# A diffusion transformer block on one core: LayerNorm tile 2's statistics and transposes moved ahead of K, one K pair split, and the last store's waits reordered

## The chip, the core and the metric

One core of one Trainium2 chip. The metric is the time of one execution on the device in microseconds (us); each kernel is run several times, and the median is told. A profile is one execution; its span is some 1.4 us shorter than the time of the same run. Times within a profile count from the start of its span.

Two kinds of number come from a trace here. Starts and durations of instructions are as the profile's views give them. Completions ("done") and landings are the semaphore updates in the trace, counted against the program's own order: every instruction of this kernel adds one to its engine's semaphore, and every transfer adds sixteen to its own. The n-th update therefore names its instruction. That is finer than the merged views and was needed for differences of a tenth of a microsecond.

## The reference

```python
B, N, D = (2, 256, 1152)          # 512 tokens in 4 tiles of 128; F = 4608, 2 heads of 576
mod = (_silu(c) @ w_mod).reshape(B, 6, 1, D)
shift_a, scale_a, gate_a, shift_m, scale_m, gate_m = [mod[:, i] for i in range(6)]
h = _layernorm(x, axis=-1) * (1 + scale_a) + shift_a
qkv = (h @ wqkv).reshape(B, N, 3, H, Dh)
# attention, wo, gate, second LayerNorm and modulation, two MLP matmuls with GELU, gate   [cut]
```

The change touches only the first line of h, the start of K, and the last store.

## The kernel before

The program is written in units with a small scheduler. TensorE and the store queue follow source order; VectorE and ScalarE follow a fixed list for the head. An instruction waits for exactly what it reads or overwrites; PSUM, the memory that TensorE writes to, is tracked by bank. Weights come in slices in a fixed order on one queue: x of both batches, three slices of the scale weights for feature blocks 0 to 3 (called slices 0, 1, 2 here), the first four rows of K's weights, three slices of the scale weights for blocks 4 to 8 (the second half), the other five K rows, and so on.

LayerNorm statistics: tiles 1 and 2 on VectorE, tiles 0 and 3 on ScalarE, the power -0.5 on GpSimd, the normalization (xn) on VectorE:

```python
def ln_stats_dve(src, chunks, bn_t, mv_t, rstd_t, tag):      # tiles 1, 2
    # three bn_stats, bn_aggr, + EPS on VectorE                              [cut]
    pool(650, ... tensor_tensor(out=rstd_t, in0=var, in1=NHALF, op=ALU.pow), "rstd_" + tag)
# ln_stats_act: tiles 0, 3: sum and square sum on ScalarE, variance, the same power  [cut]
```

TensorE ahead of K. `warm` is a matmul of 512 columns without use (in the profile of before the first ones start some 427 ns apart, from 6.74 on 216); `xn_T` transposes a normalized tile, `sca` sums one slice of the scale (three rows of weights, twelve matmuls of two columns), `hk` multiplies K's operand by the scale:

```python
XB = [(4, 5, 3), (6, 5, 7)]            # PSUM banks of the transposes, by batch
KB = [(0, 1, 2, 3), (4, 5, 6)]         # PSUM banks of the K pairs
        xn_T(1)
        warm(1, "c")
        sca(0, 3)
        xn_T(0)
        warm(1, "d")
        sca(3, 6)
        warm(1, "e")
        sca(6, 9)
        hk(0, 0)
        # ...                                                                [cut]
        xn_T(3, 0, 8)
        k_first(0)                     # a round of K: 8 matmuls of 256 columns
        k_first(1)
        xn_T(3, 8, 9)
        xn_T(2)
        # k_first(2), k_first(3), hk of batch 1, two K pairs of batch 1      [cut]
        sc_ones(KC, KT)
        k17(0, 0, KC)                  # four matmuls of K's last column block
        for kt in range(KT):
            mod_kt(WSC, kt, 0, "scb_%d" % kt, (KC, KT))     # second-half scale sums
        hk(KC, 0)
        # ...                                                                [cut]
        k_pair(range(KC), 2, 1)        # 8 matmuls; then the second half of K
```

The last store first waits for the oldest stores, then for VectorE:

```python
                    if ins is last_out:
                        for o in outs[:-4]:
                            eng_handle.wait_ge(dma_sems[o.dma_sem], o.dma_val)
                    for (k, v) in waits[ins.gidx]:
                        # wait for it                                        [cut]
```

Of the kernel before, what the change touches and what calls it, by code (L numbers as in the profile page):

```python
# [171 lines left out]
class Sched:  # L172
# [225 lines left out]
    def emit(self, nc, sems, dma_sems):  # L398
        order = self.order
        eidx = {e: 0 for e in ENGINES}  # L400
        dma_cnt = [0] * len(dma_sems)
        n_other = getattr(self, "n_other_dma_sems", 8)
        n_sp = len(dma_sems) - n_other
        di = 0
        dj = 0
        for e in ENGINES:
            for u in order[e]:
                for ins in u.instrs:
                    if u.dma_bytes > 0:
                        if e == "sp":  # L410
                            k = di % n_sp
                            di += 1
                        else:
                            k = n_sp + dj % n_other
                            dj += 1
                        dma_cnt[k] += 16
                        ins.dma_sem = k
                        ins.dma_val = dma_cnt[k]
                    else:
                        eidx[e] += 1  # L420
                        ins.eidx = eidx[e]
        self.final_counts = dict(eidx)
        self.final_dma = list(dma_cnt)
        snap = {}
        stats = {"waits": 0}

        def sem_of(d):
            if d.dma_sem is not None:
                return ("d", d.dma_sem), d.dma_val
            return ("e", d.unit.eng), d.eidx  # L430

        allu = sorted(self.units, key=lambda u: (u.start, u.uid))
        known = {e: {} for e in ENGINES}
        waits = {}
        for u in allu:
            e = u.eng
            kn = known[e]
            for ins in u.instrs:
                need = {}
                for d in ins.deps:  # L440
                    k, v = sem_of(d)
                    if need.get(k, 0) < v:
                        need[k] = v
                wl = []
                for k, v in sorted(need.items(), key=lambda kv: (-kv[1], str(kv[0]))):
                    if kn.get(k, 0) >= v:
                        continue
                    wl.append((k, v))
                    kn[k] = v
                    for d in ins.deps:  # L450
                        if sem_of(d) == (k, v):
                            sn = snap.get(d.gidx)
                            if sn:
                                for kk, vv in sn.items():
                                    if kn.get(kk, 0) < vv:
                                        kn[kk] = vv
                            break
                waits[ins.gidx] = wl
                stats["waits"] += len(wl)
                snap[ins.gidx] = dict(kn)  # L460
        self.wait_stats = stats

        outs = [ins for u in order["sp"] for ins in u.instrs if ins.is_out]
        last_out = outs[-1]

        def run_engine(e, eng_handle):
            for u in order[e]:
                for ins in u.instrs:
                    if ins is last_out:
                        for o in outs[:-4]:  # L470
                            eng_handle.wait_ge(dma_sems[o.dma_sem], o.dma_val)
                    for (k, v) in waits[ins.gidx]:
                        if k[0] == "d":
                            eng_handle.wait_ge(dma_sems[k[1]], v)
                        else:
                            eng_handle.wait_ge(sems[k[1]], v)
                    bi = ins.fn(eng_handle)
                    if ins.dma_sem is not None:
                        bi.then_inc(dma_sems[ins.dma_sem], 16)
                    else:  # L480
                        bi.then_inc(sems[e], 1)
            if e == "sp":
                for o in outs[-4:-1]:
                    eng_handle.wait_ge(dma_sems[o.dma_sem], o.dma_val)
                eng_handle.wait_ge(dma_sems[last_out.dma_sem], last_out.dma_val)

        for e, eng in (("sp", nc.sync), ("pe", nc.tensor), ("act", nc.scalar), ("dve", nc.vector), ("pool", nc.gpsimd)):
            run_engine(e, eng)
# [12 lines left out]
KT = 9  # L501
# [8 lines left out]
KC = 4  # L510
# [3 lines left out]
def c_mm(n):  # L514
    return max(n / 2.4 + 2.5, 27.0)
# [26 lines left out]
def build_kernel(nc, x, c, wqkv, wo, w_mod, w_fc1, w_fc2, out):  # L542
    S = Sched()
# [4 lines left out]
    with (  # L548
# [10 lines left out]
        def ps32(bank, c0=0, n=512):  # L559
            return psum[:, bank * 512 + c0: bank * 512 + c0 + n]  # L560
# [47 lines left out]
        Q4B = sb(O_Q4B, 1024)  # L608
# [18 lines left out]
        IDENT = sb(misc(256), 256)  # L627
# [59 lines left out]
        def mm(o, l, r, st, sp, **kw):  # L687
            S.instr(lambda e: e.matmul(o, lhsT=l, rhs=r, start=st, stop=sp, **kw), reads=[l, r], writes=[o])  # L688
# [73 lines left out]
                [xt, m, rs], [xn], "xn_%d" % t)  # L762


        XB = [(4, 5, 3), (6, 5, 7)]

        def xslot(b, kt, n=256):
            return ps16(XB[b][kt // 4], (kt % 4) * 256 + (512 if kt == 8 and b == 1 else 0), n)
# [2 lines left out]
        def xn_T(t, ka=0, kb=KT):  # L771
            b = t // 2
            S.unit("pe", (kb - ka) * c_mm(128), "xnT_%d_%d" % (t, ka))
            for kt in range(ka, kb):
                tr(xslot(b, kt)[:, (t % 2) * 128:(t % 2) * 128 + 128], XN[:, t, kt * 128:(kt + 1) * 128], IDENT)
# [5 lines left out]
        def warm(n, tag, behind=None):  # L781
            for i in range(n):
                S.unit("pe", 300.0, "warm_%s_%d" % (tag, i))
                mm(ps32(2), IDENT, Q4B, True, True)
                if behind:
                    S.instrs[-1].deps.update(j for j in S.instrs[:-1] if j.name == behind)

        def mod_kt(W, kt, col0, name, fs=(0, 9)):
            S.unit("pe", (fs[1] - fs[0]) * 27.0, name)
            for f in range(*fs):  # L790
                mm(ps32(7, col0 + f * 2, 2), W[:, kt, f * 128:(f + 1) * 128], ST[:, kt:18:9], False, kt == KT - 1, skip_group_check=True)
# [16 lines left out]
        def k_mm(kts, j, b, bank, half):  # L808

            for kt in kts:  # L810
                mm(ps32(bank, half * 256, 256), WK[:, kt, j * 128:(j + 1) * 128], HK[:, kt, b * 256:(b + 1) * 256], kt == 0 and half == 0,
                   kt == KT - 1, skip_group_check=True)

        KB = [(0, 1, 2, 3), (4, 5, 6)]
        ev_rr = [0]

        def k_pair(kts, i, b, bank=None):
# [25 lines left out]
        for n, behind in ((1, "bn_ln1_1_1"), (1, "aggr_ln1_1"), (2, "veps_ln1_1"), (2, "rstd_ln1_1")):  # L843
            warm(n, behind, behind)
        xn_T(1)
        warm(1, "c")
        sca(0, 3)
        xn_T(0)
        warm(1, "d")
        sca(3, 6)  # L850
        warm(1, "e")
        sca(6, 9)
        hk(0, 0)
        sc1a(0, KC)
# [7 lines left out]
        def k_first(kt):  # L862
            for i in range(4):
                k_pair((kt,), i, 0)

        k_first(0)
        k_first(1)
        xn_T(3, 8, 9)
        xn_T(2)
        xn_T_copy(1, 4, 8, "act")  # L870
        xn_T_copy(1, 8, 9, "act")
        for kt in range(2, KC):
# [6 lines left out]
        def k17(b, ka, kb):  # L879
            S.unit("pe", (kb - ka) * c_mm(256), "k17_%d_%d" % (b, ka))  # L880
            for kt in range(ka, kb):
                mm(ps32(7, 256 * (1 - b), 256), WK[:, kt, D - P:D], HK[:, kt, b * 256:(b + 1) * 256], b == 1 and kt == 0, kt == KT - 1,
                   skip_group_check=True)

        sc_ones(KC, KT)
        k17(0, 0, KC)
        for kt in range(KT):
            mod_kt(WSC, kt, 0, "scb_%d" % kt, (KC, KT))
        hk(KC, 0)
        sc1a(KC, KT)  # L890
        for kt in range(KC, KT):
            for b in range(2):
                if kt > KC or b:
                    hk(kt, b)
        k_pair(range(KC), 2, 1)
        for kt in range(KT):
            dma(WQ[:, kt, :], wqkv_v[:, kt, 0:D], P * D * 2, "ld_wq%d" % kt, run=2304)
            dma(WSM[:, kt, :], wmod_v[:, kt, 4 * D:5 * D], P * D * 2, "ld_sm%d" % kt, run=2304)
# [43 lines left out]
        for kt in range(KT):  # L942
            for b in range(2):
# [5 lines left out]
                else:  # L949
# [4 lines left out]

        S.first = {
            "dve": ["zq4b", "c_half", "c_silu", "bn_ln1_1_0", "bn_ln1_1_1", "bn_ln1_1_2", "aggr_ln1_1", "veps_ln1_1", "bn_ln1_2_0",
                    "xn_1", "bn_ln1_2_1", "xn_0", "bn_ln1_2_2", "aggr_ln1_2", "var_ln1_3", "veps_ln1_2", "xn_3", "hk_0_0", "sc1a_0", "hk_1_0",
                    "xn_2", "hk_0_1", "hk_1_1", "hk_2_1", "hk_3_1", "hk_%d_0" % KC, "sc1a_4", "hk_%d_1" % KC] + ["hk_%d_%d" % (kt, b) for kt in range(KC + 1, KT) for b in range(2)],
            "act": ["ld_c", "c_tanh", "sum_ln1_0", "sq_ln1_0", "sum_ln1_3", "sq_ln1_3", "xnT_cp0_4", "xnT_cp0_8", "hk_2_0", "hk_3_0",
                    "xnT_cp1_4", "xnT_cp1_8"],  # L960
        }
# [293 lines left out]
        for t in range(4):  # L1255
            b = t // 2
# [3 lines left out]
            for (c0, c1) in pieces:  # L1260
                w = c1 - c0
                S.unit("pe", JT * c_mm(w), "fc2_%d_%d" % (t, c0))
                o = ps32(acc_bank(), 0, w)
# [8 lines left out]
        by = {u.name: u for u in S.units}  # L1272
# [1 line left out]
            if u.eng == "dve" and u.name.startswith("h2T_3"):  # L1274
                S.order_after(by["gm_0_0"], u)
        S.order_after(by["gm_1_0"], by["gm_0_8"])
        S.order_after(by["rstd_ln1_2"], by["rstd_ln1_3"])
        for u in S.units:
            if u.eng == "dve" and u.name.startswith("hx_"):
                S.order_after(by["sm_0_0"], u)  # L1280
# [64 lines left out]
```

## Time and profile before

| | before |
|---|---|
| time, median of 3 runs | 244.39 us (244.12 to 244.48) |
| span of the profile | 243.0 us |
| TensorE busy | 238.2 us (98%) |
| slice 1, slice 2 landed | 9.54, 10.75 |
| first K matmul | 11.80 |
| third slice of the second half landed | 18.53 |
| first matmul of the second half of K | 20.16 |
| VectorE's last update, last store starts | 241.333, 241.431 |

TensorE is the bound almost throughout. In such a profile the only things worth looking for are TensorE's waits, and work on it that could be done while it waits. The lines are in the prediction.

### The profile page before, as it was taken

The numbers are of one execution on the slowest core, as the hardware profiler recorded it, in microseconds if no ns is written. First come the engines' busy times: TensorE is split into PE (matmuls) and PEld (weight loads), VectorE is DVE, ScalarE is ACT, GpSimd is POOL, SyncE is SP. The second block draws the span as 40 slices with busy tenths as digits, with TensorE's granted clock in tenths as the row PEclk, the third lists the DMA queues.
The fourth block names the chain that finished last, engine by engine and source line by source line (L and its number), as shares of the span: only waits on it lengthen the run. The fifth ranks groups of instructions, "written<-read, shape, count | busy, mean of one in ns | idle before, by whom it ended". The sixth has DMA issues, their size and how long they took to land.

```text
span 243.0 us, 4065 instructions
## 1 busy us (share of the span) xinstructions
PE 238.2 (98%) x1753; PEld 148.0 (61%) x1763; DVE 120.4 (50%) x217; ACT 67.2 (28%) x136; POOL 21.5 (9%) x39
## 2 busy tenths in 40 slices
PE   7999999999999999999999999999999999999996
PEld 2698854556667666898444444444656656666575
DVE  3724379596997899789999600000022222111112
ACT  4730350345424206983233322222000000000000
POOL 1500000000021186400000000020000000000000
DMA  6999999999995999979953498011000000000000
GB/s 237 334 381 392 392 391 391 398 414 405 389 350 170 350 386 393 392 266 392 323 162 82 166 308 323 0 32 68 0 16 19 16 16 19 16 16 19 18 28 21
DMA packets 30140, 51.59 MB, mean 212 GB/s; under 512 B 1703, under 2 KB 15787, under 8 KB 30123
## 3 DMA queue, kind: packets, MB, share of 16 engines
q1 hardware_dynamic: 29680, 50.14, 57.7%
q0 software_dynamic: 416, 1.19, 1.6%
q8 instruction: 14, 0.23, 0.4%
q14 instruction: 3, 0.02, 0.0%
q10 hardware_dynamic: 27, 0.00, 0.0%
HBM read 50.14 MB, written 1.19 MB: 211 GB/s over the span
## 4 chain that ended last, share of the span: by engine, by line
PE 94%; DMA 3%; SPq 1%; issue 0%; DVE 0%
PE psum L688 93%; DMA arena<-in_w_mod_dram 3%; PE psum L691 1%; SPq L669 1%; DVE arena L805 0%; DVE arena L1268 0%; DVE arena L1269 0%
## 5 line engine op out<-in xcount | busy, mean ns | idle before, releaser
L688 PE MATMUL psum<-arena 128*128 128x384 bf16 (+12 forms) x1664 | 234.8, 307 | 2.4 <-POOL arena L711 1.5
L688 PEld LDWEIGHTS psum<-arena 128*128 128x128 bf16 (+3 forms) x1674 | 142.7, 97 | 90.6 <-issue 4.5
L1063 DVE SCALAR_TENSOR_TENSOR arena<-arena 128x1152 f32<-128x1152 bf16 x32 | 44.7, 1414 | 0.6
L1268 DVE TENSOR_TENSOR arena<-psum,arena 128x384 f32<-128x384 f32 (+3 forms) x14 | 7.0, 501 | 68.0 <-PE psum L688 68.0
L1177 ACT ACTIVATE arena<-psum 128x512 bf16<-128x512 f32 (+1 forms) x44 | 22.4, 520 | 42.7 <-PE psum L688 42.7
L683 ACT ACTIVATE arena<-psum 128x512 bf16<-128x512 f32 (+6 forms) x37 | 19.6, 550 | 38.6 <-PE psum L688 37.0
L685 DVE CAST arena<-psum 128x512 bf16<-128x512 f32 (+3 forms) x13 | 8.2, 641 | 11.4 <-PE psum L688 11.3
L669 POOL DMA_DIRECT2D dit_scratch<-arena x3 | 1.8, 617 | 115.6 <-DVE arena L685 58.8
L1145 POOL TENSOR_TENSOR arena<-arena 128x384 f32<-128x384 f32 x12 | 10.9, 914 | 11.4 <-DVE arena L1144 9.8
L1090 DVE CAST arena<-psum 72x32 bf16<-72x32 f32 x1 | 0.2, 187 | 21.3 <-PE psum L688 21.3
L739 DVE BATCH_NORM_STATS2 arena<-arena 128x6 f32<-128x384 f32 (+1 forms) x18 | 9.5, 548 | 0.1
L1150 ACT ACTIVATE arena<-arena 128x1152 bf16<-128x1152 f32 x4 | 5.3, 1344 | 11.1 <-DVE arena L1149 11.1
L1144 DVE TENSOR_TENSOR arena<-psum,arena 128x384 f32<-128x384 f32 x12 | 6.5, 552 | 1.5 <-PE psum L688 0.9
L1269 DVE TENSOR_TENSOR arena<-arena 128x384 bf16<-128x384 f32 (+3 forms) x14 | 7.0, 501 | 0.5
L691 PE MATMUL psum<-arena 128*128 128x128 bf16 (+1 forms) x89 | 7.1, 219 | 0.0
L691 PEld LDWEIGHTS psum<-arena 128*128 128x128 bf16 (+1 forms) x89 | 5.8, 98 | 2.0 <-DMA arena<-in_c_dram 0.8
L1167 ACT ACTIVATE arena<-psum,arena 128x128 bf16<-128x128 bf16 x16 | 6.0, 456 | 1.7 <-PE psum L691 1.1
L1164 DVE TENSOR_SCALAR arena<-psum,arena 128x128 bf16<-128x128 bf16 x20 | 5.4, 336 | 1.9 <-PE psum L691 1.9
L1070 DVE TENSOR_REDUCE arena<-arena 128x36 f32<-128x1152 f32 x4 | 5.4, 1346 | 0.0
L1067 DVE STREAM_TRANSPOSE arena<-arena 128x1152 f32<-128x1152 f32 x4 | 5.4, 1363 | 0.0
L993 ACT ACTIVATE arena<-psum,arena 128x256 bf16<-128x256 f32 x8 | 3.7, 473 | 1.3 <-PE psum L688 0.9
L947 ACT ACTIVATE arena<-arena 128x256 bf16<-128x256 bf16 x6 | 2.6, 498 | 3.9 <-DVE arena L941 3.9
(48 smaller groups left out, 45.8 us busy)
## 6 DMA issues: line engine op xcount, KB each, us to landing
arena<-in_w_fc_dram SPq DMA_DIRECT2D x9, 1152.0 KB, 7.5
arena<-in_w_fc_dram SPq DMA_DIRECT2D x4, 2592.0 KB, 17.4
arena<-in_wqkv_dram SPq DMA_DIRECT2D x18, 288.0 KB, 10.3
arena<-in_w_mod_dram SPq DMA_DIRECT2D x3, 1728.0 KB, 20.4
arena<-in_w_mod_dram SPq DMA_DIRECT2D x3, 864.0 KB, 13.3
arena<-in_w_mod_dram SPq DMA_DIRECT2D x9, 288.0 KB, 10.8
arena<-in_wqkv_dram SPq DMA_DIRECT2D x1, 2592.0 KB, 16.7
arena<-in_wo_dram SPq DMA_DIRECT2D x1, 2592.0 KB, 24.4
```

The source lines that it names most:

```text
L683: act(c_act(n), lambda e: e.activation(out=dst, in_=src, func=ACTF.Copy), [src], [dst], name)
L685: dve(c_dve_psum16(n) if psum16 else c_dve_psum32(n), lambda e: e.tensor_copy(dst, src), [src], [dst], name)
L688: S.instr(lambda e: e.matmul(o, lhsT=l, rhs=r, start=st, stop=sp, **kw), reads=[l, r], writes=[o])
L691: S.instr(lambda e: e.transpose(o, i_, idn), reads=[i_, idn], writes=[o])
L739: dve(550, lambda e, s=s, o=o: e.bn_stats(out=o, in_=s), [s], [o], "bn_%s_%d" % (tag, ci))
L1063: dve(1270, lambda e, w=w, s=s, acc=acc: e.scalar_tensor_tensor(out=acc, in0=w, scalar=s, in1=acc, op0=ALU.mult, op1=ALU.add), [w, s, acc] ...
L1144: dve(550, lambda e, o=o, ga=ga, x1c=x1c: e.tensor_tensor(out=x1c, in0=o, in1=ga, op=ALU.mult), [o, ga], [x1c], "wo_t1_%d_%d" % (t, ci))
L1145: S.op("pool", 930, lambda e, xs=xs, x1c=x1c: e.tensor_tensor(out=x1c, in0=x1c, in1=xs, op=ALU.add), reads=[x1c, xs], writes=[x1c], name=" ...
L1167: act(440, lambda e, o=o, dst=dst, s1=s1, s2=s2: e.activation(out=dst, in_=o, func=ACTF.Identity, scale=s1, bias=s2), [o, s1, s2], [dst], ...
L1177: act(c_act(ntok), lambda e: e.activation(out=dst, in_=o, func=ACTF.Gelu_apprx_tanh), [o], [dst], "gelu_%d_%d" % (f, tok0))
L1268: dve(c_dve_psum32(w), lambda e, o=o, gm=gm, t1=t1: e.tensor_tensor(out=t1, in0=o, in1=gm, op=ALU.mult), [o, gm], [t1], "fc2_t1_%d_%d" % ( ...
L1269: dve(c_dve_32(w), lambda e, t1=t1, x1c=x1c, ost=ost: e.tensor_tensor(out=ost, in0=t1, in1=x1c, op=ALU.add), [t1, x1c], [ost], "fc2_out_%d ...
```

## The change

The intent: do tile 2's statistics earlier, transpose tile 2 while TensorE waits for the scale weights rather than between rounds of K; give the transposes and K other PSUM banks, so that this needs no new wait; put half a K pair ahead of the last third of the second-half scale sums, so that a late slice is hidden; and order the last store's waits differently.

```diff
-                    if ins is last_out:
-                        for o in outs[:-4]:
-                            eng_handle.wait_ge(dma_sems[o.dma_sem], o.dma_val)
                     for (k, v) in waits[ins.gidx]:
                         # wait for it                                        [cut]
+                    if ins is last_out:
+                        for o in outs[:-4]:
+                            eng_handle.wait_ge(dma_sems[o.dma_sem], o.dma_val)
-        XB = [(4, 5, 3), (6, 5, 7)]
+        XB = [(4, 5, 3), (6, 2, 7)]
         # in warm():                                                         [cut]
-                mm(ps32(2), IDENT, Q4B, True, True)
+                mm(ps32(0), IDENT, Q4B, True, True)
-        KB = [(0, 1, 2, 3), (4, 5, 6)]
+        KB = [(0, 1, 5, 3), (4, 2, 6)]
         xn_T(1)
-        warm(1, "c")
         sca(0, 3)
-        xn_T(0)
         warm(1, "d")
         sca(3, 6)
-        warm(1, "e")
+        warm(1, "f", "aggr_ln1_2")
+        xn_T(0)
+        warm(1, "e", "rstd_ln1_2")
+        xn_T(2, 0, 8)
         sca(6, 9)
         # ...                                                                [cut]
         k_first(0)
+        xn_T(3, 8, 9)
+        xn_T(2, 8, 9)
         k_first(1)
-        xn_T(3, 8, 9)
-        xn_T(2)
         # ...                                                                [cut]
+        def k12(half):
+            S.unit("pe", KC * c_mm(256), "k1_2%d" % half)
+            k_mm(range(KC), 4 + half, 1, KB[1][2], half)
         for kt in range(KT):
+            if kt == 6:
+                k12(0)
             mod_kt(WSC, kt, 0, "scb_%d" % kt, (KC, KT))
         # ...                                                                [cut]
-        k_pair(range(KC), 2, 1)
+        k12(1)
         # VectorE: bn_2_0, xn_1, bn_2_1, xn_0, bn_2_2 ... xn_3 ... xn_2
         #  becomes bn_2_0, bn_2_1, xn_1, bn_2_2, ..., xn_0, var_3, xn_2, xn_3   [cut]
         # GpSimd: tile 3's power after tile 2's, not the other way round        [cut]
```

More of the change, by code (lines that the diff above doesn't have):

```diff
@@ L956, in build_kernel @@
             "dve": ["zq4b", "c_half", "c_silu", "bn_ln1_1_0", "bn_ln1_1_1", "bn_ln1_1_2", "aggr_ln1_1", "veps_ln1_1", "bn_ln1_2_0",
-                    "xn_1", "bn_ln1_2_1", "xn_0", "bn_ln1_2_2", "aggr_ln1_2", "var_ln1_3", "veps_ln1_2", "xn_3", "hk_0_0", "sc1a_0", "hk_1_0",
-                    "xn_2", "hk_0_1", "hk_1_1", "hk_2_1", "hk_3_1", "hk_%d_0" % KC, "sc1a_4", "hk_%d_1" % KC] + ["hk_%d_%d" % (kt, b) for kt in range(KC + 1, KT) for b in range(2)],
+                    "bn_ln1_2_1", "xn_1", "bn_ln1_2_2", "aggr_ln1_2", "veps_ln1_2", "xn_0", "var_ln1_3", "xn_2", "xn_3", "hk_0_0", "sc1a_0", "hk_1_0",
+                    "hk_0_1", "hk_1_1", "hk_2_1", "hk_3_1", "hk_%d_0" % KC, "sc1a_4", "hk_%d_1" % KC] + ["hk_%d_%d" % (kt, b) for kt in range(KC + 1, KT) for b in range(2)],
             "act": ["ld_c", "c_tanh", "sum_ln1_0", "sq_ln1_0", "sum_ln1_3", "sq_ln1_3", "xnT_cp0_4", "xnT_cp0_8", "hk_2_0", "hk_3_0",
@@ L1276, in build_kernel @@
         S.order_after(by["gm_1_0"], by["gm_0_8"])
-        S.order_after(by["rstd_ln1_2"], by["rstd_ln1_3"])
+        S.order_after(by["rstd_ln1_3"], by["rstd_ln1_2"])
         for u in S.units:
```

## The prediction

Recorded texts, here and below, are cut where they cite what no trace or run of this case shows; the cuts are marked. No term of the sum is among them: it came to +0.50 (K's start) - 0.445 (transposes) + 0.21 (split) - 0.08 (last store), about +0.19 us, each worked out from the trace of before. Among the rivals B expected a lower granted clock after the idle of 0.51.

> **What bounds the kernel now.** I read the page first, then the chain that ended last, then the busy time of each engine in stretches of the first 14 us (where the change lies), then single instructions in narrow windows of the timeline. The page:
>
> ```profile
> PE 238.2 (98%) x1753; PEld 148.0 (61%) x1763; DVE 120.4 (50%) x217; ACT 67.2 (28%) x136; POOL 21.5 (9%) x39
> ...
> PE 94%; DMA 3%; SPq 1%; issue 0%; DVE 0%
> ```
>
> TensorE is busy 98% of 243.0 us and makes 94% of the chain. So what TensorE gains or loses in the head should arrive at the end unchanged, unless a wait in between swallows it. The chain in order of time (start us, us, what):
>
> ```profile
> 2.87 7.88 DMA arena<-in_w_mod_dram
> 10.75 0.05 issue
> 10.79 0.47 PE psum L688 x12
> 11.26 0.14 PE psum L691 x2
> 11.39 0.36 DVE arena L805
> 11.75 0.05 issue
> 11.80 1.92 PE psum L688 x16
> 13.72 0.56 PE psum L691 x10
> ...
> 240.84 0.24 DVE arena L1268
> 241.07 0.02 issue
> 241.10 0.23 DVE arena L1269
> ```
>
> The reader is to see three things. K (L688 at 11.80) starts when the third slice of the scale weights has landed (10.75), twelve two-column matmuls have summed it, and VectorE has multiplied the first K operand (L805, 0.36 us). After two rounds of K there are ten transposes on the chain, 0.56 us: the ones that the change wants ahead of K. And the end is one VectorE instruction that the last store waits for. The stretches (busy us of each engine, with counts):
>
> ```profile
> 8.75:9.07 0.32, 0.32 (x13) 0.31 (x12) 0.32 (x2) 0.32 (x1) 0.19 (x1) 1.00 1.06 318
> 9.07:9.57 0.50, 0.50 (x15) 0.50 (x12) 0.45 (x2) 0.47 (x2) 0.00 (x0) 1.00 0.97 346
> 9.57:9.79 0.22, 0.17 (x4) 0.11 (x2) 0.14 (x2) 0.02 (x1) 0.00 (x0) 1.00 1.14 374
> 9.79:10.11 0.32, 0.32 (x13) 0.32 (x12) 0.08 (x2) 0.32 (x1) 0.22 (x1) 1.00 0.94 357
> 10.33:10.79 0.46, 0.15 (x1) 0.00 (x1) 0.32 (x1) 0.46 (x2) 0.46 (x2) 1.00 1.01 383
> 13.55:14.11 0.56, 0.56 (x12) 0.56 (x10) 0.00 (x0) 0.00 (x0) 0.00 (x0) 1.00 1.03 376
> ```
>
> These cut TensorE's queue by unit: 12 scale matmuls are 0.32 us, nine transposes 0.50, one warming matmul 0.22 (the rows 8.75, 9.07, 9.57). At 10.33 the queue is empty until 10.79: 0.46 us is the whole slack ahead of K. The two places outside the head that matter, from the timeline on VectorE and from the store queue's own waits:
>
> ```profile
> 19.81 0.29 DVE L805 TENSOR_SCALAR arena<-arena,psum 128x256 bf16<-128x256 bf16 x1 [4.37 <-PE psum L688]
> ```
> ```profile
> SPq L669 <- DVE arena L1269: 95.8, 13, 37.2
> ...
> SPq L476 <- DVE arena L1269: 0.5, 1, 0.5
> ```
>
> Thirteen stores wait for VectorE in the transfer itself; the fourteenth, the last, waits in a separate semaphore instruction ahead of it.
>
> [...] transposes start 55.8 ns apart, warming matmuls 216, two-column matmuls 26.7. [...] the semaphore updates of the 45 second-half scale matmuls, counted against program order, come 34.2 ns apart while the matmuls start 26.7 ns apart, so the semaphore falls about 0.34 us behind. [...]
>
> **The change, part by part.** All times below in us from the span's start; landings and completions are semaphore updates in the trace of before.
>
> 1) The VectorE order. The three statistics of tile 2 no longer alternate with the normalizations. Chaining the measured durations (0.46 between statistics, 0.24 aggregate, 0.15 epsilon, 0.58 a normalization): tile 1 normalized at about 7.95 (7.80 before), tile 0 at 9.38 (8.82), tile 2 at 10.32 (12.70), tile 3 at 11.06 as before, since that waits for ScalarE's square sum (9.55), a subtraction and a 0.55 power on GpSimd. Tile 1's transposes start at 8.04 anyway, behind the warming matmuls. None of this is a new wait on TensorE.
>
> 2) The TensorE order ahead of K. Transposes of tile 1: 8.04 to 8.54. Scale slice 0 follows at once, as one warming matmul is gone: to 8.86. One warming matmul: to 9.08. Now slice 1 is wanted, which landed at 9.54 (before, it was first used at 9.79): with 0.045 from landing to start, 9.585. TensorE idles 0.51. Then scale matmuls 0.32 (9.905), warming 0.215 (10.12), nine transposes of tile 0 0.50 (10.62), warming 0.215 (10.835), eight transposes of tile 2 0.445 (11.28). Only now slice 2, which has been there since 10.747. Before, its first matmul ran at 10.79. From that start to K's start the trace has 1.005 (matmuls and their lagging semaphore 0.567 to completion, 0.025 to VectorE, 0.365 multiplication, 0.045 to TensorE); I add 0.015 for semaphore lag behind the transposes. K starts at 12.30 instead of 11.80: **+0.50**. The eight transposes of tile 3 stay hidden in this gap (11.60 to 12.05).
>
> 3) In K, eight of the ten transposes at 13.55 are gone: 8 x 0.0558 = **-0.445**. Parts 2 and 3 together: about +0.06. The work was moved out of a full stretch, but into a stretch whose slack was before another landing.
>
> 4) The split K pair. Before: nine units of five scale matmuls, then eight K matmuls (8 x 0.109 = 0.87), which cover the semaphore lag, VectorE's multiplication (start 19.81, done 20.11) and 0.047 back to TensorE (20.157); the stall there was about 0.02. After, with +0.06: scale matmuls from 18.13 to 18.93, four K matmuls to 19.36, fifteen scale matmuls with the last start at 19.74, four K matmuls to 20.20. The four K matmuls in the middle let the semaphore catch up, but the fifteen behind them let it fall back by about 0.1: completion at 20.05, against 19.93 without a lag. VectorE needs 0.326 to done (20.38), TensorE 0.047: 20.425. Only 0.44 of K now covers this, so about 0.2 is stall. Against 20.157 before: **+0.27** for the head in all. The split would pay if the last second-half slice came late; it landed at 18.53 and was used at 18.87 before and at about 19.36 after, so it pays nothing here.
>
> 5) PSUM banks: K pair 2 of batch 0 goes to bank 5, that the copy of tile 0 and 1 must leave first. The copy would start near 10.85 and take 1.02; K wants the bank at 12.74. Hidden. The others have more.
>
> 6) The last store. Before, ten old stores' waits were put ahead of VectorE's, and the compiler paired them up such that VectorE's wait sat in the last pair (241.350) and the transfer started at 241.431, 0.097 after VectorE's update at 241.334. In the changed order VectorE's wait is first in the list, the place of the wait that the transfer itself carries now. Then the transfer should follow as the earlier stores do, 0.015 to 0.018 behind: **-0.08**.
>
> Sum: +0.50 - 0.445 + 0.21 - 0.08 = about +0.19 us.
>
> **The rivals.** A: the intended gain. If slack ahead of K were long enough for eight transposes, the change would give -0.445 - 0.08 and the split would hide a late slice: 243.9. For it: the idle at 10.33. Against: 0.46 of slack was not free for all of it, as slice 1 comes only at 9.54 and two warming matmuls (0.43) now stand in the full stretch. It would come true where the slices land about half a microsecond later than in this trace. [...] the column of granted clock is 1.00 with gaps of 0.3 to 0.4 too. C: a later wait swallows everything. TensorE waits for weights nowhere after 11 us; the second-half weights of K land 0.9 ahead of use and more later, Q's rows 1.9 to 3.6 ahead. So no absorber, and the time is as computed: 244.6. D: the scale semaphore does not bind as computed (lag gone): 0.1 less, 244.45.
>
> **Range and chances.** I take the sum and shade it slightly to A, since a landing later by a few tenths helps only the changed kernel: **244.55 us**. The three runs of before spread over 0.36 us, the disputed terms over about half a microsecond: 244.1 to 244.9 holds 8 in 10. Two per cent is 4.9 us, ten times all terms together: faster 0.01, same 0.98, slower 0.01.
>
> **What would show it.** Step 2: an idle of about 0.5 just before 9.6, waiting for the modulation weights, and K's first 256-column matmul at 12.3; if it starts by 11.9, A is right. Step 3: two transposes between the rounds of K instead of ten. Step 4: VectorE's first second-half multiplication near 20.1 and a gap of about 0.2 on TensorE after it; no gap makes it wrong. Step 6: no separate wait between VectorE's last instruction and the last store. A clock column under 1.00 near 10 would be B.

## The result, and the profile after

The changed kernel: 244.56 us median (244.32 to 244.9, 6 runs); before, in the same rounds and earlier, 244.35 us (244.12 to 244.81, 6 runs). The ratio is 1.0007, with a 95% interval of 0.9994 to 1.002: the same. Ratios here are the mean time of one kernel's fast runs over that of the other's of the same rounds, so not quite the ratio of the medians.

The page of the changed kernel:

```profile
PE 238.7 (98%) x1753; PEld 148.1 (61%) x1763; DVE 120.3 (49%) x217; ACT 67.0 (28%) x136; POOL 21.5 (9%) x39
...
PE 98%; DVE 0%; issue 0%; POOL 0%; POOLq 0%
```

TensorE's share of the chain has gone from 94 to 98%: the transfer of slice 2, 7.88 us of the chain before, is no longer on it. The counts are the same, as the work is. Its chain of waits in order of time (start us, us, what):

```profile
9.16 0.91 PE psum L688 x25
10.07 0.08 issue
10.14 0.66 PE psum L691 x9
10.81 0.22 PE psum L688
11.02 0.45 PE psum L691 x8
11.47 0.30 PE psum L688 x12
11.77 0.16 PE psum L691 x3
11.93 0.36 DVE arena L805
12.29 0.05 issue
12.33 1.05 PE psum L688 x8
13.38 0.11 PE psum L691 x2
13.49 6.62 PE psum L688 x95
20.11 0.29 DVE arena L805
20.41 0.05 issue
20.45 13.26 PE psum L688 x144
```

The reader is to see, from the top: tile 0's nine transposes, a warming matmul and tile 2's eight transposes follow one another on the chain, then slice 2's twelve sums. K starts at 12.33 instead of 11.80. Two transposes (13.38) stand in K where there were ten. And a new step has come onto the chain at 20.11: VectorE's first second-half multiplication, with K behind it at 20.45 instead of 20.16. The store queue's own waits of the changed kernel:

```profile
SPq L669 <- DVE arena L1276: 96.2, 14, 37.2
```

All fourteen stores now wait for VectorE in the transfer itself. VectorE's last update is at 241.63 and the last store starts 0.016 behind it; before it was 0.098.

So the sum of the profiles is: first K matmul +0.53; eight transposes out of K -0.45; second half of K +0.21, together +0.29 at its first matmul (20.451 against 20.157); the same from there to the last matmul; last store -0.08; net +0.21 at the start of the last store.

### The profile page after: what moved, and what is told of

It is laid out like the page before. It is cut to its first block, busy times and chain, and to the rows that moved or that the text cites. A ratio compares the mean times of both kernels' runs of the same rounds, so it can differ in the third digit from the quotient of the medians.

```text
span 243.2 us, 4065 instructions
## 1 busy us (share of the span) xinstructions
PE 238.7 (98%) x1753; PEld 148.1 (61%) x1763; DVE 120.3 (49%) x217; ACT 67.0 (28%) x136; POOL 21.5 (9%) x39
## 4 chain that ended last, share of the span: by engine, by line
PE 98%; DVE 0%; issue 0%; POOL 0%; POOLq 0%
PE psum L688 96%; PE psum L691 2%; DVE arena L805 0%; POOL arena L711 0%; DVE arena L1275 0%; DVE arena L1276 0%; POOL arena L710 0%; POOL arena L717 0%; POOL arena L715 0%; POOLq L1337 0%
## 5 line engine op out<-in xcount | busy, mean ns | idle before, releaser
L743 POOL TENSOR_TENSOR arena<-arena 128x1 f32<-128x1 f32 x6 | 3.6, 596 | 1.7 <-DVE arena L742 1.7
```

## The experiments

Each is the whole kernel with the edit named. "K" is the start of the first K matmul, "third round to second half" is the time from the completion of the first matmul of K's third round to that of the first matmul of its second half. No landing ahead of K moved this interval (6.02 in e5, e6, e9 and e13, with slice 2 landing anywhere from 10.27 to 11.04); a late third slice of the second half did, in e1, e11 and e12. Diffs are against the kernel before or the changed kernel, as said. The runs are four jobs (e1 to e4, e5 to e8, e9 and e11, e12 and e13), each on a chip of its own; whether part of the scatter of landings between jobs comes from the chip was not tested.

| run | slice 1 landed | slice 2 landed | K | third round to second half | time, median | before, same job | ratio, 95% |
|---|---|---|---|---|---|---|---|
| before (profile) | 9.54 | 10.75 | 11.80 | 6.05 | | | |
| changed (profile) | 9.55 | 10.67 | 12.33 | 6.26 | 244.56 | 244.35 | 1.0007, 0.9994 to 1.002 |
| e1 | 9.12 | 10.55 | 11.60 | 6.35 | 244.34 | 244.29 | 1.0005, 0.9993 to 1.0017 |
| e2 | 9.57 | 10.76 | 11.83 | 6.26 | 244.39 | 244.29 | 1.0007, 0.9995 to 1.0019 |
| e3 | 9.18 | 10.78 | 12.18 | 6.05 | 244.21 | 244.29 | 1.0002, 0.999 to 1.0014 |
| e4 | 9.07 | 10.41 | 11.91 | 6.26 | 244.21 | 244.29 | 0.9999, 0.9987 to 1.0011 |
| e5 | 9.64 | 10.72 | 11.77 | 6.02 | 244.32 | 244.44 | 0.9997, 0.9984 to 1.0009 |
| e6 | 9.59 | 10.98 | 12.05 | 6.02 | 244.17 | 244.44 | 0.9993, 0.9979 to 1.0006 |
| e7 | 9.13 | 10.51 | 12.15 | 6.27 | 244.3 | 244.44 | 0.9995, 0.9982 to 1.0007 |
| e8 | 10.02 | 11.03 | 12.80 | 6.26 | 244.58 | 244.44 | 1.0002, 0.9989 to 1.0016 |
| e9 | 8.80 | 10.27 | 12.12 | 6.02 | 244.25 | 244.35 | 0.9994, 0.9982 to 1.0007 |
| e11 | 9.41 | 10.70 | 11.90 | 6.58 | 244.2 | 244.35 | 0.9991, 0.9977 to 1.0005 |
| e12 | 8.99 | 10.29 | 12.14 | 6.10 | 244.31 | 244.24 | 0.9999, 0.9986 to 1.0011 |
| e13 | 9.74 | 11.04 | 12.23 | 6.02 | 244.18 | 244.24 | 0.9991, 0.9977 to 1.0005 |

No interval excludes 1, so the times settle nothing here; they only bound everything to a few tenths of a per cent. What settles things is in the intervals of the traces. Profiles with the same order in K agree there to 0.01 where no slice came late (6.05 in two, 6.26 to 6.27 in five, 6.02 in four). Another interval is the same in all fourteen profiles: from the completion of the second half's first matmul to that of the last matmul of the kernel it is 220.36 us, and 0.52 from there to VectorE's last update. Nothing that happens in the head is taken back or added to later.

### e1: the store's waits alone

Against the kernel before: the diff's first two hunks alone, the waits for the old stores moved behind VectorE's.

> The kernel before with only the order of the last store's waits changed. Theory (my sum): the transfer follows VectorE's last update by about 0.016 us instead of 0.097, span and time 0.08 us less; the head is as before (first K matmul near 11.8, first second-half K matmul near 20.16). Rival: the old stores' waits, now emitted after VectorE's, run behind it on the critical tail: five wait instructions of about 0.07 us, time 0.3 to 0.4 us more.

VectorE's last update was at 241.43 and the store started at 241.44, 0.02 behind it, with the five wait instructions done at 240.99. The rival falls: emitted later, they still run earlier. (In the traces of before and of the changed kernel, of the last store's eleven waits the one written first stands with the transfer, and the other ten in pairs in five instructions. In before, four of these start 0.06 to 0.07 apart and the fifth, at 241.350, has VectorE's wait; in the changed kernel all five are past at 241.20, ahead of VectorE's last update at 241.63.) The theory holds for the start of the store; the time did not show 0.08 (the spread of single runs is 0.7). The transfer's landing scatters more than this gain: 1.69 us from start to landing here, 1.42 before. The profile also showed something that I had not asked for; its chain:

```profile
7.29 11.64 DMA arena<-in_w_mod_dram
18.93 0.05 issue
18.98 40.54 PE psum L688 x315
```

The third second-half slice landed at 18.93, 0.4 later than in the kernel before, while K was 0.2 earlier. TensorE waited for it, and the interval from K's third round was 6.35 instead of 6.05. That is the case that the split was made for. Its own interval, 6.26 (e2), would have been 0.09 shorter, which is an estimate: no run has the split and so late a slice.

### e2: the split alone

```diff
+        def k12(half):
+            S.unit("pe", KC * c_mm(256), "k1_2%d" % half)
+            k_mm(range(KC), 4 + half, 1, KB[1][2], half)
         for kt in range(KT):
+            if kt == 6:
+                k12(0)
             mod_kt(WSC, kt, 0, "scb_%d" % kt, (KC, KT))
-        k_pair(range(KC), 2, 1)
+        k12(1)
```

> The kernel before with only the K pair split in the scale sums. Theory (too little K left to cover the scale semaphore and VectorE's multiplication): gap of 0.2 us on TensorE after the second half of the pair, first second-half K matmul at 20.35 to 20.40 instead of 20.16, time 0.2 us more. Rival (the split hides the late third slice of the second half): that matmul at 20.16 or earlier, time the same or less. Rival (the lag drains entirely in the first half): gap of 0.1 us at most.

The interval is 6.26 instead of 6.05, with K at 11.83: the split costs 0.21 by itself. TensorE's gap before the second half of K is 0.34 start to start, instead of 0.13. The chain of this run:

```profile
20.05 0.29 DVE arena L805
20.34 0.05 issue
20.39 39.27 PE psum L688 x292
```

The multiplication and the way back are on the chain, as in the changed kernel. Both rivals fall in this trace, in which the third slice landed at 18.64.

### e3: the changed kernel with the pair whole

Against the changed kernel: e2's diff in reverse.

> The changed kernel with the K pair whole again after the scale sums. Theory: first K matmul at 12.33 as in the changed kernel, gap ahead of the second-half K at most 0.04, first second-half K matmul at 20.20 to 20.25 instead of 20.45; time 0.2 us less than the changed kernel, so 0.0 to 0.1 us under the kernel before. Rival (the split is neutral and something else in the head made the loss): that matmul stays near 20.45.

The interval is 6.05 again, as before. K started at 12.18 instead of 12.33, and the second half at 20.09; the 0.15 between them and my numbers is K's start, not the pair. (K started 3.00 after slice 1 here. The chain of this run goes through tile 3, as in e6 below: its power took 0.87, it was normalized at 11.67, and its transposes ran up to K.) The split's 0.21 is thus shown from both sides.

### e4: without the two warming matmuls

```diff
-        warm(1, "f", "aggr_ln1_2")
         xn_T(0)
-        warm(1, "e", "rstd_ln1_2")
         xn_T(2, 0, 8)
```

> The changed kernel without the two warming matmuls behind slice 1. Theory (the stretch from slice 1's landing to K is full, so each costs its 0.215): first K matmul at 11.85 to 11.95 instead of 12.33, second-half K at 20.0 to 20.05, time 0.43 less than the changed kernel, 0.2 less than before. Rival (a landing or VectorE's tile 2 sets K's start): K no earlier than 12.2. [...]

K started at 11.91, 0.42 earlier than in the changed kernel, and the second half at 20.03. The granted clock of the profiled run was 0.999 and matmuls in K stayed 0.109 apart, so the two warming matmuls were not needed for that here. But slice 1 landed at 9.07 here, 0.48 earlier than in the changed kernel's profile, so part of the 0.42 could be that. And the chain runs through tile 3 in this run (see e6), so it was no longer the queue between slice 1 and K that set the start. The number fits; that each warming matmul costs its 0.215 is not shown by this pair of profiles alone.

### e5: K's last column block between the scale rows

The split's gain without its cost: fill the place between the scale rows with four matmuls that stood ahead of the sums, and leave all eight of the pair behind them.

```diff
-        k17(0, 0, KC)
         for kt in range(KT):
+            if kt == 6:
+                k17(0, 0, KC)
             mod_kt(WSC, kt, 0, "scb_%d" % kt, (KC, KT))
```

> The kernel before with one edit: the four matmuls of K's last column block, which stood ahead of the second-half scale sums, stand between their sixth and seventh rows (like the split's first half, but taken from ahead of the sums, so that all eight of the K pair stay behind). Theory (increments lag behind two-column matmuls; longer matmuls let them catch up): the last scale matmul's completion comes 0.3 us after its start instead of 0.54, no gap ahead of the second-half K, from the third round of K to the second-half K 6.02 us instead of 6.05, and a third slice landing as late as 18.95 is hidden (in the store-order run it cost 0.3). Rival (a fixed latency, no lag): completion stays 0.5 us behind the start.

The last scale matmul was done 0.32 after its start, instead of 0.54; VectorE's multiplication was done at 19.85 and K wanted it at 20.11; no gap; the interval 6.02. All as the lag theory has it. In the trace of before, the semaphore updates of the 45 two-column matmuls come 34.2 ns apart, the matmuls 26.6. The last one's completion after its start: in the kernel before and in e3, where the 45 run in a row, 0.54; with longer matmuls ahead of the last 15, 0.32 (changed kernel, e2, e4 to e9, e13). A latency that doesn't depend on the run of small matmuls is ruled out. The slice landed at 18.46, so that a late one is hidden was not tried in this run. The expected 18.95 is too much, by this trace: the last fifteen scale matmuls started at 18.84, so a slice that lands after 18.79 makes TensorE wait. In e12, with the same filler, one at 18.78 cost 0.08, as K was further on there.

### e6: an improved order

Against the changed kernel: the pair whole, e5's edit, and

```diff
         sca(0, 3)
-        warm(1, "d")
+        xn_T(0)
         sca(3, 6)
-        warm(1, "f", "aggr_ln1_2")
-        xn_T(0)
-        warm(1, "e", "rstd_ln1_2")
         xn_T(2, 0, 8)
         sca(6, 9)
```

> The changed kernel with the pair whole, K's last column block between the scale rows as in the run above, no warming matmuls after slice 0, and tile 0's transposes ahead of slice 1's scale sums, so that they lie in the wait for slice 1, and tile 2's in the wait for slice 2. Theory: K's first matmul about 1.05 to 1.1 us after slice 2's landing as in the kernel before (near 11.8 to 11.9), two transposes instead of ten in K, 6.02 us from the third round to the second-half K: that matmul at 19.7 to 19.8 instead of 20.16, the last store 0.08 earlier, time 0.45 to 0.55 less than before (243.8). Rival (K's weights for the second half, landing near 18.8 to 19.7, or the late third slice take the gain back): a gap at 19.7, time less by 0.3 or less.

K started 1.07 after slice 2, two transposes stood in K, the interval was 6.02, and the store came 0.02 behind VectorE. But slice 2 landed 0.23 later than before, so K started at 12.05 and the second half at 19.94: 0.22 earlier than before, where I had said 0.4. The time was 0.27 less by the medians, half of what I expected, and the interval reaches to no difference. The chain of this run holds a second bound that I had not seen:

```profile
10.04 0.88 POOL arena L751
...
10.95 0.59 DVE arena L760
...
11.59 0.62 PE psum L691 x8
12.21 0.88 PE psum L688 x8
```

Tile 3's power on GpSimd took 0.88 us where it took 0.55 in the kernel before; so tile 3 was normalized at 11.55, and its eight transposes, which the prediction had hidden behind VectorE's multiplication, ended just at K's start. (The chain's last line starts later than the first K matmul, at 12.05, since its pieces are merged with modelled ends.)

### e7: the improved order with the split

Against the changed kernel: e6's last diff alone.

> The changed kernel, split kept, without warming matmuls after slice 0 and with tile 0's transposes ahead of slice 1's sums. Theory: K starts as in the run above (1.05 to 1.1 after slice 2's landing), 6.26 us from the third round to the second-half K as in every run with the split: 0.24 worse than the run above, 0.25 to 0.3 better than the kernel before. Rival (the split costs nothing once K starts early, as the third slice is then the bound): the same time as the run above.

The split's cost is there again: 6.27. The other half was a miss: K started 1.64 after slice 2, not 1.05, though the slice was early (10.51). The chain is that of e6: ScalarE's square sum at 9.80, GpSimd's power 0.88, tile 3 normalized at 11.64, transposes 11.69 to 12.14, K at 12.15.

### e8: the changed kernel again

> The changed kernel again, on the same chip as the three above, for a second profile and more times. Theory: time 0.1 to 0.3 more than the kernel before; K's first matmul near 12.3, or up to 0.4 earlier if slice 1 lands earlier [...]; 6.26 us from the third round to the second-half K; the last store 0.02 after VectorE.

K started at 12.80, outside what I had said. Slice 1 landed at 10.02, 0.47 later than in the first profile, and K was 0.47 later: in both profiles K starts 2.78 after slice 1's landing. The beginning of the chain, and a stretch of the windows view (us, TensorE busy, weight loads, VectorE, ScalarE, GpSimd, clock, DMA share, GB/s):

```profile
2.17 7.85 DMA arena<-in_w_mod_dram
10.02 0.05 issue
10.07 0.71 PE psum L688 x13
```
```profile
9.20:10.06 0.86, 0.04 (x1) 0.00 (x0) 0.55 (x3) 0.40 (x2) 0.71 (x2) 1.00 1.01 343
```

TensorE stands idle for 0.8 us ahead of slice 1, and everything up to K is behind it on the chain. In the kernel before, K starts 1.05 after slice 2 (also in e1 and e5, which have its order; 1.07 in e2, whose chain goes through tile 3). So the change had tied K to another landing, as long as tile 3 is not later still, as it was in e3.

### e9: tile 3's variance on GpSimd

Against e6: the one subtraction moved from VectorE to GpSimd, behind tile 2's power, so that tile 2 need not wait for it.

> The improved order (run e6) with tile 3's variance subtraction on GpSimd, so that tile 2's normalization on VectorE no longer stands behind it and thus behind ScalarE's square sum. Theory: tile 2 normalized 0.3 to 0.4 us earlier relative to tile 3, its transposes no longer the bound; K's first matmul is started by the later of two: 1.05 to 1.08 us after slice 2's landing, or some 0.5 us after tile 3 is normalized. Where slice 2 is the later, the same as run e6; time 0.3 to 0.55 less than the kernel before. Rival: GpSimd, with one instruction more ahead of tile 3's power, delays tile 3 by 0.2 or more and K with it: time as before or 0.2 less.

A miss. Tile 2 came 1.02 ahead of tile 3, as in e6 (1.02), not 0.3 more: its own power ended at 9.97 (0.81 us long), so the subtraction had not been what held it. The rival did not come true either: tile 3's power ended 1.02 after tile 2's, as in e6. K at 12.12 was set by tile 3, although slice 2 had landed as early as 10.27.

### e11: the improved order again

> The improved order (run e6) once more, on the chip of the run above. Theory: in the profile 6.02 us from the third round of K to the second-half K, eight transposes out of K, K's start 1.05 to 1.1 after slice 2's landing unless tile 2 or 3 is normalized late (then 0.06 plus 0.445 after the later one's end, more for tile 2); time 0.2 to 0.5 less than the kernel before, with the interval of five rounds reaching to about no difference. Rival (the gain in the head is lost later): matmuls between the second-half K and the last one take longer than 220.3 us, the time from one to the other in the kernel before.

K started at 11.90, 1.20 after slice 2's landing at 10.70: tile 2 was normalized at 10.37, its transposes ran to 10.87, and slice 2's sums came behind them, 0.15 later than the slice alone would have had it. Tile 3 was early (11.02), and eight transposes were gone from K. And the third second-half slice landed at 19.02, half a microsecond later than before. TensorE waited for it, in spite of the filler from e5: 6.58. Being early had turned into a wait for a transfer; the second half of K started at 20.35, 0.19 later than in the kernel before. That it is 220.36 from there to the end answers the rival.

### e12 and e13: does GpSimd's power wait for VectorE's normalization?

GpSimd's recorded ends are used in what follows: in e6 both normalizations that wait for a power started 0.03 after its recorded end. In the profiles so far, a power took 0.55 to 0.57 where VectorE ran no normalization beside it, and 0.66 to 0.89 in most where it did. Against e6, e12 puts a short VectorE instruction from later in the program between tile 3's variance and tile 2's normalization; e13 also puts one ahead of tile 0's normalization:

```diff
-  "veps_ln1_2", "xn_0", "var_ln1_3", "xn_2", "xn_3",
+  "veps_ln1_2", "qs", "xn_0", "var_ln1_3", "st32", "xn_2", "xn_3",
```

> The improved order (run e6) with one short VectorE instruction (the 18-column cast, 0.17 us, which stood at 22 us) put between tile 3's variance and tile 2's normalization. Theory (GpSimd's power waits where a VectorE normalization has started 0.1 to 0.2 us before it: 0.79 to 0.88 us in eleven such pairs of the runs so far, 0.55 to 0.69 where the normalization starts within 0.05 before it or later): the normalization starts within 0.05 of tile 3's power, the power takes 0.56 to 0.70 instead of 0.87, tile 3 is normalized at most 1.35 us after ScalarE's square sum instead of about 1.6 to 1.85, and K's start is no longer set by tile 3 where slice 2 lands after 10.6. Time 0.2 to 0.5 less than the kernel before. Rival (the power's time is scatter of the engine): it stays at 0.8 or scatters.

> The run above, and a second VectorE instruction from 22 us (a 128-to-32 reduction, 0.36 us) between tile 2's epsilon and tile 0's normalization. Theory: tile 2's power on GpSimd, 0.81 in every run with the changed order, takes 0.56 to 0.70, as tile 0's normalization now starts after it; tile 0 is normalized 0.2 to 0.3 later. K's start the same as in the run above where slice 1 or 2 sets it. Rival: the power stays at 0.81.

Tile 2's power (POOL L743) and the normalization of tile 0 (DVE L760), in e6 and then in e13:

```profile
9.09 0.81 POOL L743 TENSOR_TENSOR arena<-arena 128x1 f32<-128x1 f32 x1 [0.31 <-DVE arena L742]
8.92 0.57 DVE L760 TENSOR_SCALAR arena<-arena 128x1152 bf16<-128x1152 bf16 x1
```
```profile
9.19 0.72 POOL L743 TENSOR_TENSOR arena<-arena 128x1 f32<-128x1 f32 x1 [0.31 <-DVE arena L742]
9.30 0.58 DVE L760 TENSOR_SCALAR arena<-arena 128x1152 bf16<-128x1152 bf16 x1
```

e12 did not test what it was to test: the normalization still started 0.09 ahead of the power (0.11 in e6), as the short instruction moved it by 0.03 only; the power took 0.90. (Its interval of 6.10 is the third second-half slice, which landed at 18.78 and made TensorE wait.) e13 did, at tile 2: the normalization of tile 0 started 0.10 after the power instead of 0.17 before it, and the power took 0.72 instead of 0.81, as expected but for 0.02. Tile 3's power in the same run, with the normalization 0.08 ahead, took 0.89. Over all fourteen profiles, wherever a normalization started at least 0.08 ahead, the power took the time for which the two overlapped plus 0.40 to 0.41 (for instance 0.40 and 0.81, 0.46 and 0.87, 0.26 and 0.67). So it ended 0.40 to 0.41 after the normalization (in the changed kernel at 9.725 and 9.322, and at 8.316 and 7.905). Where the normalization started only 0.02 to 0.05 ahead, the power took 0.56 to 0.59, near the 0.55 to 0.57 that it took alone. Where the power had started 0.07 to 0.10 ahead, it took 0.68 to 0.72, 0.13 to 0.15 longer than alone, and the normalization its usual 0.58. What the runs show is these times. By what mechanism the two engines' instructions affect each other is not shown.

## Why the prediction was right

The time was 244.56, the prediction 244.55, the range 244.1 to 244.9. That is closer than the method deserves: e8 shows that a second profile of the same kernel has K 0.47 later.

- Step 1, the VectorE chain: predicted 7.95, 9.38, 10.32, 11.06 for tiles 1, 0, 2, 3; measured 7.92, 9.33, 10.35, 11.00. In the profile on record it was right. The working assumed 0.55 for tile 3's power, which held there (0.59), with the normalization beside it started only 0.02 earlier. That was luck: in eight of the ten profiles with the new VectorE order (e9, e12 and e13 have nearly that one) this power took 0.78 to 0.90. In e8 it took 0.87, and tile 3 came at 11.44. This step was right with too narrow a reason.
- Step 2, K's start: predicted 12.30, measured 12.33. The 0.51 of idle ahead of slice 1 did not appear: the warming matmuls, 427 ns apart at first, came 216 ns apart only from 7.63 on, instead of 6.74, which put tile 1's transposes at 8.50 instead of 8.04, and the queue reached slice 1 just when it landed. Slice 1's first sum started at 9.596, predicted 9.585. So the step's result held because the landing set it, and its sign (an idle of 0.5) was seen only in e8, as 0.8.
- Step 3, eight transposes out of K: predicted -0.445, measured -0.447 (first matmul to third round 1.858 instead of 2.305).
- Step 4, the split: predicted +0.21, measured +0.21, in the changed kernel and alone (e2), and taken back without it (e3). The sentence that the split pays nothing, said of a landing at 18.53, held for those at 18.06 (changed kernel) and 18.64 (e2) and is too strong in general: in e1 a slice at 18.93 cost 0.30 with the pair whole.
- Step 5, banks: no bank wait is on the chain.
- Step 6, the last store: predicted -0.08, measured -0.082, and alone in e1.
- Rival A, the intended gain: it needs slack that slice 1's landing and the two warming matmuls had taken. That later landings would bring it about, for which the prediction was shaded to A, was wrong: in e8 slices 1 and 2 landed 0.48 and 0.28 later than in the profile of before, and K started 1.77 after slice 2 instead of 1.05. With K 2.78 after slice 1, A would need slice 2 to land at least 1.73 after slice 1 (an estimate, 2.78 less 1.05); in the fourteen profiles it landed 1.01 to 1.60 after it. Rival B, a lower granted clock: it was 0.999 or 1.00 in all runs, and 1.00 in e8 around an idle of 0.8 (the window above). Rival C, that nothing later absorbs it: 220.36 us in all fourteen profiles. Rival D: the lag was as computed.

What stays open: whether e6's order is faster than the kernel before. Two jobs of five rounds gave 0.9993 and 0.9991, each with an interval that holds 1. In the traces it takes 0.45 out of K and 0.03 out of the second half's start, and 0.08 at the end; but K's start is set by whichever of slice 2 and tile 3 is later, and the second half by a slice that landed anywhere between 18.03 and 19.02 over these runs. A gain of 0.1 to 0.3 is likely, and not shown. By what rule slices land earlier or later from run to run was not studied.

## What to carry to other kernels

Moving work into a wait only pays if it fits between the same two events: here the transposes went in behind an earlier landing than the one whose slack was meant, and in front of a later one, so 0.45 saved was 0.53 paid. Before cutting a piece of cover work in two, add up what it covers, including the lag of the semaphore: here the last of 45 two-column matmuls was done 0.54 us after its start, and 0.32 with longer matmuls ahead of the last 15. Filler taken from elsewhere (e5) brought that 0.32 at no cost, with 6.02 from the third round to the second half instead of 6.05. And where landings scatter by half a microsecond, judge a change of a tenth by intervals inside the trace that no landing has moved, not by the total.
